# A decode block that streams 88 MB: three loads behind memsets, more idle products, and a scaling split the other way

## The chip, the cores and the metric

The kernel runs on one core of a Trainium2 chip. Its time is the device time of one execution in microseconds (us). Before the change it is 214.62 us, the median of three runs (214.51 to 215.23).

## The reference

One decode step, four tokens (B = 4) of width D = 448, in fp32:

```
h  = x + attention(layernorm(x))            # 16 query heads, 8 k/v heads, Dh = 256
h2 = h + W2 @ gelu(W1 @ layernorm(layernorm(h)) + b1) + b2
```

Attention uses only the last 1024 of the 4096 cached positions, per token and k/v head: `q = layernorm(x) @ wq`, `softmax(q k^T / 16) v`, then `@ wo`. The bulk of the data are the used parts of the k and v caches (each 8 heads x 4 tokens x 1024 x 256 floats, 33.5 MB), read once. With wq, wo, w1 and w2 the kernel reads 88.29 MB. Nothing is reused, so little arithmetic falls on each byte.

## The kernel before, in words

**Loads.** The host packs the inputs so that each load is one rectangle of 128 rows with long rows. Three slots of SBUF (a ring, tag "t") take them in turn. The first slot takes two loads: `first` (the weights wq of head group 0 and a transposed copy of x, 928 KB) and then the rest of `stream0` behind it (4992 KB). Eleven more loads `stream1` to `stream11` of 4 to 7 MB follow, then v of the last head group (`v7`, two parts), wo of the last two groups (`wo67`), w1 (two parts) and w2 (four parts). All of them are issued by SyncE (SP) on one DMA queue, in the order of the program. A load into a slot that was used before waits until its old content has been consumed; the first three slots are free at the start. A small load `rows` (x, b1, b2 by rows, 44 KB) is issued by ScalarE (ACT) on another queue into the tile `rs`.

**Set-up.** VectorE (DVE) and GpSimd (POOL) clear the tiles that later hold the transposed operands: `qT`, `oT` and `pT` (two of each) and `gT`, all with zeros between the used columns. POOL clears these seven in a row (L165), then `rs` (L168), behind which ACT issues `rows`.

**Attention.** For each head group g = 0..7: project q (`pq`, L199), copy it to SBUF (ACT, `qs`, L201) and transpose it with a selecting product (`pqt`, L205); scores (`s`, L219), row maximum (DVE), exponential (ACT), transpose of the probabilities (`ppt`, L244), values (`po`, L256). Then `heads`: the output of values, 128 x (2, 256) in PSUM, is scaled by the softmax's reciprocal into `o`, the first of the two halves by DVE (L273), the second by ACT (L274); four products transpose `o` (`pot`, L281), for column half c = 0, 1 and half i = 0, 1; DVE spreads the result into `oT` (L288), and `project_o` multiplies by wo (`acc` for g < 6, `hsum` for the last two).

**Tail.** From `hsum`: residual, two layer norms, the MLP's first product `pu` (L418, w1), GELU, transpose (`put`), second product `py` (L449, w2), residual, and the store of `res`.

**Idle products.** `keep_warm(n, to)` (L319 to L322) issues n products of a zero tile `idle` (bf16, 32 x 128 times 128 x 512) into a PSUM tile that is overwritten or not read. They stand in the last three head groups and in the tail, where TensorE (PE) would otherwise wait.

The order of work on TensorE is that of the program; the other engines are ordered by a scheduler.

Of the kernel before, what the change touches and what calls it, by code (L numbers as in the profile page):

```python
# [8 lines left out]
F32 = mybir.dt.float32  # L9
# [6 lines left out]
B, D = 4, 448  # L16
HQ, HKV, SK, DH = 16, 8, 4096, 256
REP = HQ // HKV
W = min(4096, max(256, SK // 4))
F = 1792  # L20
P = 128
# [8 lines left out]
WC = 4 * D  # L30
QU = KV // 4
X0 = 64
# [23 lines left out]
def width(part):  # L56
    kind, g, _ = part
    if kind in "kv":
        return QU
    return WC + (X0 if (kind, g) == ("q", 0) else 0)  # L60
# [8 lines left out]
def block_kernel(ctx: ExitStack, tc, rows, first, streams, v7, wo67, w1, w2, out):  # L69
    nc = tc.nc  # L70
# [7 lines left out]
    ps_m = ctx.enter_context(tc.tile_pool(name="ps_m", bufs=2, space=PSUM))  # L78
# [4 lines left out]
    def slot(name):  # L83
        return ring.tile([P, SLOT], F32, tag="t", name=name)

    held = {}
    streams_first = streams[0]

    def part(kind, g, i=0):
        while (kind, g, i) not in held:  # L90
            src = streams.pop(0)
            t = slot("stream")
            wanted = LOADS[len(LOADS) - len(streams) - 1]
            if src is streams_first:
                nc.sync.dma_start(t[:, : WC + X0], first)  # L95
            at = WC + X0 if src is streams_first else 0
            nc.sync.dma_start(t[:, at : at + src.shape[-1]], src)  # L97
            at = 0
            for one in wanted:
                held[one] = t[:, at : at + width(one)]  # L100
                at += width(one)
        return held[kind, g, i]
# [55 lines left out]
    qT = [const.tile([P, 2, B, Q], F32, name=f"qT{i}") for i in range(2)]  # L158
    pT = [const.tile([P, NKC // 2, B, Q], F32, name=f"pT{i}") for i in range(2)]
    oT = [const.tile([P, 4, Q], F32, name=f"oT{i}") for i in range(2)]  # L160
    gT = const.tile([P, NFC, Q], F32, name="gT")
    idle = const.tile([P, 512], BF16, name="idle")
    nc.vector.memset(idle, 0.0)
    for t in qT + oT + pT + [gT]:
        nc.gpsimd.memset(t, 0.0)  # L165

    rs = const.tile([P, 2 * P + FQ], F32, name="rs")
    nc.gpsimd.memset(rs, 0.0)  # L168
# [2 lines left out]
    def spread(t):  # L171
        return t[..., ::GAP]
# [23 lines left out]
    def project_q(g, parts):  # L196
        pq = ps_m.tile([P, 512], F32, tag="m", name=f"pq{g}")
        for j, a, cols, w in parts:
            nc.tensor.matmul(pq[j * Q : (j + 1) * Q, cols], yT[:, a, :], w, start=True, stop=True)  # L199
        qs = work.tile([P, 512], F32, tag="qs", name=f"qs{g}")  # L200
        nc.scalar.copy(qs, pq)  # L201

        pt = ps_m.tile([P, 2 * REP, B], F32, tag="m", name=f"pqt{g}")
        for i in range(2 * REP):
            nc.tensor.matmul(pt[:, i, :], qs[:, i * P : (i + 1) * P], sel[:, :B], start=True, stop=True)  # L205

        src = pt.rearrange("p (r c) b -> p c b r", r=REP)
        for i in range(2):
            nc.vector.tensor_copy(qT[g % 2][:, :, :, i * REP : (i + 1) * REP], src)  # L209

    def scores(g):
        s = [ps_s.tile([P, 512], F32, tag="s", name=f"s{g}_{h}") for h in range(2)]
        if g == HKV - 1:
            keep_warm(12, s[0])
        mx = work.tile([P, 2], F32, tag="mx", name=f"mx{g}")
        for h in range(2):
            for c in range(2):
                for b in range(B):
                    nc.tensor.matmul(  # L219
                        s[h][b * Q : (b + 1) * Q, :], qT[g % 2][:, c, b, :], load_k(g, h, c)[:, b, :],  # L220
                        start=(c == 0), stop=(c == 1),
                    )
            nc.vector.reduce_max(mx[:, h : h + 1], s[h], axis=AX.X)  # L223
        nm = work.tile([P, 1], F32, tag="nm", name=f"nm{g}")
        nc.vector.tensor_max(nm, mx[:, 0:1], mx[:, 1:2])
        nc.vector.tensor_scalar_mul(nm, nm, -SCALE)  # L226
        p = work.tile([P, 2 * 512], F32, tag="p", name=f"p{g}")
        sums = work.tile([P, 2], F32, tag="sums", name=f"sums{g}")
        for h in range(2):
            nc.scalar.activation(  # L230
                p[:, h * 512 : (h + 1) * 512], s[h], AF.Exp, bias=nm, scale=SCALE,
                accum_out=sums[:, h : h + 1],
            )
        rec = work.tile([P, 1], F32, tag="rec", name=f"rec{g}")
        nc.vector.tensor_add(rec, sums[:, 0:1], sums[:, 1:2])
        nc.vector.reciprocal(rec, rec)
        return p, rec

    def transpose_p(g, p):
        pt = ps_t.tile([P, NKC, P], F32, tag="t", name=f"ppt{g}")  # L240
        if g == HKV - 1:
            keep_warm(8, pt.rearrange("p c k -> p (c k)"))
        for c in range(NKC):
            nc.tensor.transpose(pt[:, c, :], p[:, c * P : (c + 1) * P], ident)  # L244

        src = pt.rearrange("p (c i) (b q) -> p c i b q", i=2, b=B)
        for i in range(2):
            nc.vector.tensor_copy(pT[g % 2][:, :, :, i * REP : (i + 1) * REP], src[:, :, i, :, :REP])  # L248
# [21 lines left out]

    def heads(g, po, rec):
        o = work.tile([P, 2, DH], F32, tag="o", name=f"o{g}")
        nc.vector.tensor_scalar_mul(o[:, 0], po[:, 0], rec)  # L273
        nc.scalar.mul(o[:, 1], po[:, 1], rec)  # L274
        pt = ps_m.tile([P, 512], F32, tag="m", name=f"pot{g}")
        if g >= HKV - 3:
            keep_warm(2, pt)
        pt = pt[:, : 2 * REP * B].rearrange("p (c r b) -> p c r b", c=2, r=REP)
        for c in range(2):
            for i in range(2):  # L280
                nc.tensor.matmul(  # L281
                    pt[:, c], o[:, i, c * P : (c + 1) * P], rows_of_pair[:, i * REP : (i + 1) * REP, :],
                    start=(i == 0), stop=(i == 1),
                )
        if g >= HKV - 2:
            keep_warm(1)
        dst = oT[g % 2].rearrange("p (r c) q -> p c r q", r=REP)
        nc.vector.tensor_copy(spread(dst), pt)  # L288
# [30 lines left out]
    def keep_warm(n, to=None):  # L319
        to = tail[0][:, 0, :] if to is None else to  # L320
        for _ in range(n):
            nc.tensor.matmul(to[:Q, :512], idle[:, :Q], idle, start=True, stop=True)  # L322


    p, rec = scores(0)
    project_q(1, wq_parts(part("q", 1)))
    transpose_p(0, p)
    for g in range(HKV):
        if g + 1 < HKV:
            p, rec_next = scores(g + 1)  # L330
            if g + 2 < HKV:
                project_q(g + 2, wq_parts(part("q", g + 2)))
            transpose_p(g + 1, p)
            if g + 1 == HKV - 2:
                keep_warm(8, ps_m.tile([P, 512], F32, tag="m", name="wait"))
            if g + 1 == HKV - 1:
                tail.append(ps_t.tile([P, 2, 512], F32, tag="t", name="tail"))
                accs = once.tile([P, D], F32, tag="u", name="accs")
                nc.scalar.copy(accs, acc)
                keep_warm(10)  # L340
                hsum = ps_s.tile([P, 512], F32, tag="s", name="hsum")[:, :P]
                ph = hsum.rearrange("p (i c) -> p i c", i=2)
                pu = ps_s.tile([P, 512], F32, tag="s", name="pu")[:, :FQ]
                for j in range(4):
                    nc.tensor.matmul(ph[j * Q : (j + 1) * Q], sel, columns(accs, j), start=True, stop=False)
        else:
            v7t = load_v7()
            tw = slot("w1")
            wo_last = [wo_rows(tw[:, i * WC : (i + 1) * WC]) for i in range(2)]
            nc.sync.dma_start(tw[:, : 2 * WC], wo67)  # L350
            tw1 = tw[:, 2 * WC : 2 * WC + W1C]
            for a, n in ((0, 2 * F), (2 * F, W1C - 2 * F)):
                nc.sync.dma_start(tw1[:, a : a + n], w1[:, a : a + n])
            tw2 = slot("w2")
            for c0, n in ((0, 8), (8, 3), (11, 2), (13, 1)):
                nc.sync.dma_start(tw2[:, c0 * D : (c0 + n) * D], w2[:, c0 * D : (c0 + n) * D])  # L356
        if g == HKV - 1:
            keep_warm(4)
        po = values(g, v7t if g == HKV - 1 else None)
        heads(g, po, rec)  # L360
        if g < HKV - 2:
            project_o(g, wo_rows(part("o", g)))
        if g == HKV - 1:
            keep_warm(3)
            for i in range(2):
                project_o(HKV - 2 + i, wo_last[i])
        if g + 1 < HKV:
            rec = rec_next
# [24 lines left out]
    m = row_mean(hs, pm[:, 0:1], "m")  # L393
# [4 lines left out]
    m = row_mean(ds, pm2[:, 0:1], "m2")  # L398
# [128 lines left out]
```

## Time and profile before

| what | value |
|---|---|
| median of three runs | 214.62 us (214.51 to 215.23) |
| the profiled execution: own time / span | 214.47 us / 212.7 us |
| TensorE busy | 147.9 us (70%) |
| VectorE, ScalarE, GpSimd busy | 33.5, 24.1, 5.6 us |
| moved by DMA | 88.52 MB, mean 416 GB/s |
| mean granted TensorE clock | 0.864 |

The span is the profiled part of the execution; 1.8 us of its own time lie outside. Times in the profile are counted from the span's start. In rows of the time-ordered view the columns are: start, duration, engine, line, operation, output<-input, partitions x elements and type, number of instructions, and in brackets how long the engine had been idle before and what ended that. PEld is TensorE loading weights, which overlaps its products. SPq is SyncE issuing a DMA. In the table of stretches a row gives: stretch, its length, busy time and number of instructions for PE, PEld, DVE, ACT and POOL, the granted clock, the mean busy share of the 16 DMA engines, and GB/s. A DMA packet is counted there in the stretch in which it starts, so that a short stretch can show a share above 1, or 0.

### The profile page before, as it was taken

The numbers are of one execution on the slowest core, as the hardware profiler recorded it, in microseconds if no ns is written. First come the engines' busy times: TensorE is split into PE (matmuls) and PEld (weight loads), VectorE is DVE, ScalarE is ACT, GpSimd is POOL, SyncE is SP. The second block draws the span as 40 slices with busy tenths as digits, with TensorE's granted clock in tenths as the row PEclk, the third lists the DMA queues.
The fourth block names the chain that finished last, engine by engine and source line by source line (L and its number), as shares of the span: only waits on it lengthen the run. The fifth ranks groups of instructions, "written<-read, shape, count | busy, mean of one in ns | idle before, by whom it ended". The sixth has DMA issues, their size and how long they took to land.

```text
span 212.7 us, 2616 instructions
## 1 busy us (share of the span) xinstructions
PE 147.9 (70%) x1143; PEld 65.7 (31%) x1143; DVE 33.5 (16%) x138; ACT 24.1 (11%) x57; POOL 5.6 (3%) x17
## 2 busy tenths in 40 slices
PE   0476825842890896870798770687989898999994
PEld 0342311410420622330324130143352434426443
DVE  1410310400112001310104110031130031101220
ACT  1110200300002100210003000030030102000310
POOL 6100000000000000000000000000000000000110
PEclk9999985995578569997559996589699999999999
DMA  7899797989989899998999989999999999999992
GB/s 299 384 466 508 339 508 339 501 383 460 478 367 474 381 466 430 416 481 356 487 392 466 455 384 461 434 434 384 436 411 444 425 434 425 410 417 423 427 386 74
DMA packets 3355, 88.52 MB, mean 416 GB/s; under 512 B 384, under 2 KB 640, under 8 KB 1040
## 3 DMA queue, kind: packets, MB, share of 16 engines
q1 hardware_dynamic: 3312, 88.31, 97.0%
q8 instruction: 9, 0.15, 0.3%
q10 hardware_dynamic: 32, 0.05, 0.1%
q14 instruction: 2, 0.02, 0.0%
HBM read 88.29 MB, written 0.07 MB: 415 GB/s over the span
## 4 chain that ended last, share of the span: by engine, by line
DMA 76%; PE 19%; ACT 1%; DVE 1%; SPq 1%; issue 1%; ACTq 0%
DMA stream<-stream 65%; DMA w<-w 11%; PE s L219 7%; PE po L256 6%; PE ppt L244 2%; PE pq L199 2%; PE pqt L205 1%; PE tail L322 1%; ACT qs L201 1%; PE py L449 0%; ACT p L230 0%; SPq L356 0%; DVE mx L223 0%; SPq L97 0%; SPq L95 0%
## 5 line engine op out<-in xcount | busy, mean ns | idle before, releaser
L219 PE MATMUL s<-stream,qT 128*32 128x512 f32 x256 | 39.3, 762 | 17.8 <-DMA stream<-stream 17.8
L256 PE MATMUL po<-stream,pT 128*32 128x512 f32 x224 | 29.9, 674 | 15.3 <-DMA stream<-stream 15.3
L219 PEld LDWEIGHTS s<-stream,qT 128*32 128x32 f32 x256 | 10.3, 138 | 44.1 <-issue 32.3
L223 DVE TENSOR_REDUCE mx<-s 128x1 f32<-128x512 f32 x16 | 11.1, 692 | 61.5 <-PE s L219 61.5
L256 PEld LDWEIGHTS po<-stream,pT 128*32 128x32 f32 x224 | 6.9, 119 | 31.9 <-DMA stream<-stream 17.9
L199 PE MATMUL pq<-stream,yT 128*32 128x512 f32 (+1 forms) x80 | 10.7, 630 | 7.7 <-DMA stream<-stream 4.8
L281 PE MATMUL pot<-ident,o 128*128 128x8 f32 x64 | 11.3, 287 | 4.7 <-DVE o L273 3.7
L205 PE MATMUL pqt<-sel,qs 128*128 128x4 f32 x64 | 10.1, 281 | 6.1 <-ACT qs L201 6.1
L281 PEld LDWEIGHTS pot<-ident,o 128*128 128x128 f32 x64 | 10.0, 223 | 13.0 <-DVE o L273 11.3
L201 ACT COPY qs<-pq 128x512 f32<-128x512 f32 x8 | 4.7, 586 | 79.5 <-PE pq L199 79.5
L230 ACT ACTIVATE p<-s,nm 128x512 f32<-128x512 f32 x16 | 10.9, 689 | 15.8 <-DVE nm L226 15.8
L205 PEld LDWEIGHTS pqt<-sel,qs 128*128 128x128 f32 x64 | 9.4, 225 | 10.7 <-ACT qs L201 10.7
L273 DVE TENSOR_SCALAR o<-po,rec 128x256 f32<-128x256 f32 x8 | 3.9, 484 | 52.9 <-PE po L256 52.9
L274 ACT ACTIVATE o<-po,rec 128x256 f32<-128x256 f32 x8 | 3.8, 474 | 68.8 <-DVE o L273 68.8
L244 PE MATMUL ppt<-ident,p 128*128 128x128 f32 x64 | 9.8, 299 | 0.4 <-ACT p L230 0.4
L199 PEld LDWEIGHTS pq<-stream,yT 128*32 128x32 f32 x80 | 4.4, 128 | 15.6 <-issue 14.6
L293 PE MATMUL acc<-stream,oT 128*32 128x448 f32 x48 | 7.6, 709 | 2.2 <-DVE oT L288 1.4
L322 PE MATMUL tail<-idle 128*32 128x512 bf16 x33 | 8.5, 381 | 0.4 <-DVE pT L248 0.4
L322 PEld LDWEIGHTS <-idle 128*32 128x32 bf16 x67 | 5.8, 96 | 9.3 <-issue 3.9
L244 PEld LDWEIGHTS ppt<-ident,p 128*128 128x128 f32 x64 | 8.1, 162 | 1.4 <-ACT p L230 1.1
L193 POOL TENSOR_TENSOR r<-ve_r,mhalf 128x1 f32<-128x1 f32 x2 | 1.1, 542 | 191.7 <-DVE ve_r L192 191.7
L209 DVE COPY qT<-pqt 128x16 f32<-128x16 f32 x16 | 2.1, 171 | 20.7 <-PE pqt L205 20.7
(98 smaller groups left out, 70.0 us busy)
## 6 DMA issues: line engine op xcount, KB each, us to landing
stream<-stream SPq DMA_DIRECT2D x5, 7040.0 KB, 40.4
stream<-stream SPq DMA_DIRECT2D x2, 6912.0 KB, 40.6
stream<-stream SPq DMA_DIRECT2D x2, 4992.0 KB, 25.1
stream<-stream SPq DMA_DIRECT2D x2, 4096.0 KB, 24.0
stream<-stream SPq DMA_DIRECT2D x1, 5888.0 KB, 34.4
w<-w SPq DMA_DIRECT2D x2, 1792.0 KB, 23.1
v<-v SPq DMA_DIRECT2D x1, 3072.0 KB, 19.8
w<-wo SPq DMA_DIRECT2D x1, 1792.0 KB, 20.1
```

Source lines behind the costliest of these rows:

```text
L199: nc.tensor.matmul(pq[j * Q : (j + 1) * Q, cols], yT[:, a, :], w, start=True, stop=True)
L201: nc.scalar.copy(qs, pq)
L205: nc.tensor.matmul(pt[:, i, :], qs[:, i * P : (i + 1) * P], sel[:, :B], start=True, stop=True)
L219: nc.tensor.matmul(s[h][b * Q : (b + 1) * Q, :], qT[g % 2][:, c, b, :], load_k(g, h, c)[:, b, :], start=(c == 0), stop=(c == 1),)
L223: nc.vector.reduce_max(mx[:, h : h + 1], s[h], axis=AX.X)
L230: nc.scalar.activation(p[:, h * 512 : (h + 1) * 512], s[h], AF.Exp, bias=nm, scale=SCALE, accum_out=sums[:, h : h + 1],)
L244: nc.tensor.transpose(pt[:, c, :], p[:, c * P : (c + 1) * P], ident)
L256: nc.tensor.matmul(po[b * Q : (b + 1) * Q], pT[g % 2][:, c, b, :], vt[:, :, b, :], start=(c == 0), stop=(c == NKC // 2 - 1),)
L273: nc.vector.tensor_scalar_mul(o[:, 0], po[:, 0], rec)
L281: nc.tensor.matmul(pt[:, c], o[:, i, c * P : (c + 1) * P], rows_of_pair[:, i * REP : (i + 1) * REP, :], start=(i == 0), stop=(i == 1),)
L293: nc.tensor.matmul(acc[i * Q : (i + 1) * Q, :], oT[g % 2][:, i, :], wt[:, i, :], start=(g == 0), stop=(g == HKV - 3),)
L322: nc.tensor.matmul(to[:Q, :512], idle[:, :Q], idle, start=True, stop=True)
```

## The change

Three things are done in one change:

1. The three slots of the ring are taken at the start, and `first` is issued at once. In each slot POOL sets one element to zero, at the place where the slot's next load begins. The loads `stream0`, `stream1` and `stream2` thereby wait for POOL. The memset for `stream0` comes after those of `qT`, `oT` and the first `pT`; the two others after the second `pT` and `gT`. (In the diff, "second to fourth load" are these three, `first` being the first.)
2. Idle products: 3 before the transposes of q of the last head group, 10 for 8 before the transposes of its probabilities, 3 for 2 in each of the last three `heads`, 6 for 4 before the last `values`; and 10 after the last transposes of probabilities become 2 into a tile of their own and 8.
3. In `heads`, DVE scales the first 128 columns of both halves, ACT the last 128 columns of both.

```diff
@@ part @@
             src = streams.pop(0)
-            t = slot("stream")
+            t = first_slots.pop(0) if first_slots else slot("stream")
             wanted = LOADS[len(LOADS) - len(streams) - 1]
-            if src is streams_first:
-                nc.sync.dma_start(t[:, : WC + X0], first)
@@ set-up @@
     nc.vector.memset(idle, 0.0)
-    for t in qT + oT + pT + [gT]:
+    first_slots = [slot("stream") for _ in range(3)]
+    nc.sync.dma_start(first_slots[0][:, : WC + X0], first)
+    for t in qT + oT + pT[:1]:
         nc.gpsimd.memset(t, 0.0)
+    for t, at in zip(first_slots, (WC + X0, 0, 0)):
+        nc.gpsimd.memset(t[:1, at : at + 1], 0.0)
+        if t is first_slots[0]:
+            for later in pT[1:] + [gT]:
+                nc.gpsimd.memset(later, 0.0)
@@ project_q @@
-        pt = ps_m.tile([P, 2 * REP, B], F32, tag="m", name=f"pqt{g}")
+        pt = ps_m.tile([P, 512], F32, tag="m", name=f"pqt{g}")
+        if g == HKV - 1:
+            keep_warm(3, pt)
+        pt = pt[:, : 2 * REP * B].rearrange("p (a b) -> p a b", b=B)
@@ transpose_p @@
-            keep_warm(8, pt.rearrange("p c k -> p (c k)"))
+            keep_warm(10, pt.rearrange("p c k -> p (c k)"))
@@ heads @@
-        nc.vector.tensor_scalar_mul(o[:, 0], po[:, 0], rec)
-        nc.scalar.mul(o[:, 1], po[:, 1], rec)
+        nc.vector.tensor_scalar_mul(o[:, :, :P], po[:, :, :P], rec)
+        nc.scalar.mul(o[:, :, P:], po[:, :, P:], rec)
         pt = ps_m.tile([P, 512], F32, tag="m", name=f"pot{g}")
         if g >= HKV - 3:
-            keep_warm(2, pt)
+            keep_warm(3, pt)
@@ the loop over head groups @@
             if g + 1 == HKV - 1:
+                keep_warm(2, ps_m.tile([P, 512], F32, tag="m", name="wait"))
                 tail.append(ps_t.tile([P, 2, 512], F32, tag="t", name="tail"))
...
-                keep_warm(10)
+                keep_warm(8)
...
         if g == HKV - 1:
-            keep_warm(4)
+            keep_warm(6)
```

How it moves instructions, at the places the prediction speaks of. SyncE at the start of the program, before (`first` is the input named so, `stream` the big loads; the last row shown is the fifth load, which waits for its slot):

```order
L95 DMA stream<-first 128x1856
L97 DMA stream<-stream 128x9984
L97 DMA stream<-stream 128x14080 x2
L97 DMA stream<-stream 128x13824 [waits DMAHW0_49,DMAHW1_49,DVE_49,PE_49]
```

and now:

```order
L163 DMA stream<-first 128x1856
L95 DMA stream<-stream 128x9984 [waits Pool_49]
L95 DMA stream<-stream 128x14080 [waits Pool_49] x2
L95 DMA stream<-stream 128x13824 [waits DMAHW0_49,DMAHW1_49,DVE_49,PE_49]
```

The order is the same; the three loads behind `first` have got a wait for POOL. What POOL does up to there now (`stream` is the single element in a slot):

```order
L165 MEMSET oT_117 128x128
L165 MEMSET pT_114 128x512
L167 MEMSET stream 1x1
L170 MEMSET pT_115 128x512
L170 MEMSET gT 128x448
L167 MEMSET stream 1x1 x2
L173 MEMSET rs 128x704
```

Three one-element memsets have come in between; the order of the others is kept. TensorE in `heads` of the last head group, before (`po` is the output of values, `pot` the transpose of `o`):

```order
L256 MATMUL po_909<-v_893,pT_115 32x512 x3
L322 LDWEIGHTS idle
L322 MATMUL pot_929<-idle 32x512
L322 LDWEIGHTS idle
L322 MATMUL pot_929<-idle 32x512
L281 MATMUL pot_929<-ident,o_926 128x8 [waits DVE_49]
L281 MATMUL pot_929<-ident,o_926 128x8 [waits Activation_49]
L281 MATMUL pot_929<-ident,o_926 128x8 x2
```

and now:

```order
L264 MATMUL po_922<-v_904,pT_115 32x512 x3
L330 LDWEIGHTS idle
L330 MATMUL pot_942<-idle 32x512
L330 LDWEIGHTS idle
L330 MATMUL pot_942<-idle 32x512
L330 LDWEIGHTS idle
L330 MATMUL pot_942<-idle 32x512
L289 MATMUL pot_942<-ident,o_939 128x8 [waits DVE_49]
L289 MATMUL pot_942<-ident,o_939 128x8
L289 MATMUL pot_942<-ident,o_939 128x8 [waits Activation_49]
L289 MATMUL pot_942<-ident,o_939 128x8
```

One idle product more, and two of the four transposes instead of one stand ahead of the wait for ACT.

## The prediction

> **What bounds the kernel now.** I read the page first: the engines' busy time and instructions, the DMA queues (packets, MB, share of the 16 DMA engines) and issues (KB each, us to landing).
>
> ```profile
> PE 147.9 (70%) x1143; PEld 65.7 (31%) x1143; DVE 33.5 (16%) x138; ACT 24.1 (11%) x57; POOL 5.6 (3%) x17
> q1 hardware_dynamic: 3312, 88.31, 97.0%
> q8 instruction: 9, 0.15, 0.3%
> stream<-stream SPq DMA_DIRECT2D x5, 7040.0 KB, 40.4
> stream<-first SPq DMA_DIRECT2D x1, 928.0 KB, 4.8
> rs<-rows ACTq DMA_DIRECT2D x1, 44.0 KB, 7.3
> out<-res SPq DMA_DIRECT2D x1, 64.0 KB, 1.5
> ```
>
> The loads occupy the 16 DMA engines for 97% of the span. A table of stretches shows where the other 3% lie (last two numbers of a row: share of the DMA engines, GB/s):
>
> ```profile
> 1.40:1.60 0.20, 0.00 (x0) 0.00 (x0) 0.20 (x1) 0.00 (x0) 0.20 (x2) 1.00 0.00 0
> 1.60:1.80 0.20, 0.00 (x0) 0.00 (x0) 0.06 (x1) 0.00 (x0) 0.20 (x2) 1.00 1.87 223
> 1.60:3.60 2.00, 0.00 (x0) 0.00 (x0) 0.06 (x1) 0.00 (x0) 2.00 (x7) 1.00 0.79 241
> 20.00:207.00 187.00, 136.67 (x1027) 58.51 (x1022) 28.98 (x110) 22.20 (x55) 1.08 (x2) 0.84 1.00 428
> 208.00:209.00 1.00, 0.96 (x35) 0.69 (x30) 0.00 (x0) 0.00 (x0) 0.00 (x0) 1.00 0.47 163
> ```
>
> From 20 to 207 us the share is 1.00 at 428 GB/s. What is lost lies at the two ends: before the first packets at 1.6 to 1.8, in a slow first 2 us, and in the last 2, where by 208 to 209 half of the engines have finished and the others have not. The chain of waits puts TensorE between the loads, which misleads. Two links near its end:
>
> ```profile
> 183.96 0.33 SPq L356
> 184.80 24.08 DMA w<-w
> ```
>
> SyncE issues w2 when TensorE has freed its slot at 183.96. But 24.08 us pass until it lands, and w2's 3136 KB take 3.21 MB / 428 GB/s = 7.5 us: for some 16.6 us the load stood behind others. The 7040 KB loads say the same: 7.21 MB / 428 GB/s = 16.8 us, and 40.4 us to landing. So these issues could come some 16 us later without harm, and a faster TensorE brings no byte sooner. The end follows the last bytes:
>
> ```profile
> 208.92 0.37 PEld L449 LDWEIGHTS py<-w,gT 128*32 128x32 f32 x16 [0.31 <-DMA w<-w]
> 209.49 0.16 PEld L449 LDWEIGHTS py<-w,gT 128*32 128x32 f32 x8 [0.20 <-DMA w<-w]
> ```
>
> `py` waits twice for w2, 0.31 + 0.20 us; without these waits it would end 0.51 us sooner, so TensorE follows the DMA closely, and the final part of w2 (used at 209.49) sets the end. The price of an edit is therefore what it does to the moment at which the DMA engines run dry.
>
> **The change part by part.** *The waits at the start.* Rows of POOL, SyncE and TensorE, in order of time:
>
> ```profile
> 0.31 0.10 POOL L515 MEMSET const-bfloat16-1.0<- 128x1 bf16 x1
> 0.74 0.36 SPq L95 DMA_DIRECT2D stream<-first  x1
> 1.15 1.71 SPq L97 DMA_DIRECT2D stream<-stream  x3
> 2.00 0.99 POOL L165 MEMSET pT<- 128x512 f32 x2
> 2.94 0.47 POOL L165 MEMSET gT<- 128x448 f32 x1
> 3.35 0.68 POOL L168 MEMSET rs<- 128x704 f32 x1
> 4.07 0.57 ACTq L169 DMA_DIRECT2D rs<-rows  x1
> 5.62 0.57 PE L178 MATMUL pm_x<-stream,mean 128*128 128x12 f32 x2 [5.62 <-DMA stream<-first]
> ```
>
> The first `pT` is done at 2.00 + 0.99/2 = 2.50. A memset of one element isn't in the trace; the nearest row, 128x1, takes 0.10, and below it stands nothing but 0. From POOL's end to a waiting queue's issue: `rs` ends at 3.35 + 0.68 = 4.03 and ACT issues at 4.07, so 0.04. `stream0` is issued at about 2.65 instead of 1.15, 1.5 us later.
>
> Does a DMA engine run dry by it? `first` was issued at 0.74 and its packets begin between 1.60 and 1.80: 0.9 to 1.1 us. The packets of `stream0` can then begin at 3.5 to 3.8. The engines still have `first` until then: its 928 KB are 0.95 MB, and the stretch up to 4.4 reads:
>
> ```profile
> 1.60:4.40 2.80, 0.00 (x0) 0.00 (x0) 0.06 (x1) 0.00 (x0) 2.44 (x7) 1.00 0.88 306
> ```
>
> 2.8 us at 306 GB/s are 0.86 MB of packets begun: at 4.4 there is still some of `first` left. That leaves 0.6 to 0.9 us of cover, and the wait costs nothing. Beyond the cover each microsecond would cost one microsecond, since nothing later catches it up.
>
> Queued behind the waiting instruction on SyncE are `stream1` and `stream2`, released after `gT`: 2.94 + 0.47 + three small memsets, about 3.7, and issued at 3.75 and 4.1. They are needed when 0.95 + 5.11 MB have passed, 14 us after 1.7. POOL's `rs` and with it `rows` move by at most 0.3 us; `rs` is read in the tail, at 196 us. So 0 here.
>
> Can it gain? In the first 2 us the engines move 241 GB/s instead of 428, a shortfall of 0.37 MB or 0.87 us. This is where SyncE hands three big loads to the same engines (1.15 to 2.86). If these hinder `first`, the change frees up to 0.87 us; if the engines merely start slowly, nothing. No row tells the two apart, since no load of this trace starts alone. The bounds are -0.87 and 0; I take -0.1, near 0, because the same SyncE instruction shows no such dip when the first of the five of this merged row is issued at 25.04 into running transfers:
>
> ```profile
> 25.04 69.79 SPq L97 DMA_DIRECT2D stream<-stream  x5
> 24.00:26.00 2.00, 1.29 (x17) 0.59 (x9) 1.01 (x3) 0.95 (x2) 0.00 (x0) 1.00 1.04 451
> ```
>
> One rule of the Trainium skill speaks against the edit: "DMA: Bandwidth & Descriptors", section "Rules for kernel authors", has DMAs issued early, so that their fixed set-up cost overlaps, and its section "Anatomy of one DMA" puts that cost, for DMAs issued by GpSimd, at about 2.0 us, most of it at the end, in the confirmation of the last write. If all 2.0 us lay ahead of the data, the packets of `stream0` would begin at 4.65, and the time by that, an estimate, would be up to 0.3 us more. The trace, with 0.9 to 1.1 us from issue to packets, doesn't agree with so much ahead.
>
> *The idle products and the split.* In `heads` of the last group:
>
> ```profile
> 191.02 0.59 PE L322 MATMUL pot<-idle 128*32 128x512 bf16 x2
> 191.28 0.48 DVE L273 TENSOR_SCALAR o<-po,rec 128x256 f32<-128x256 f32 x1 [5.16 <-PE po L256]
> 191.82 0.39 PE L281 MATMUL pot<-ident,o 128*128 128x8 f32 x2 [0.21 <-DVE o L273]
> 191.86 0.47 ACT L274 ACTIVATE o<-po,rec 128x256 f32<-128x256 f32 x1 [6.85 <-DVE o L273]
> 192.39 0.83 PE L281 MATMUL pot<-ident,o 128*128 128x8 f32 x6 [0.18 <-ACT o L274]
> 193.16 1.04 PE L322 MATMUL tail<-idle 128*32 128x512 bf16 x4
> 194.28 0.16 PEld L299 LDWEIGHTS hsum<-w,oT 128*32 128x32 f32 x8 [0.58 <-DMA w<-wo]
> ```
>
> An idle product adds (1.04 - 0.59) / 2 = 0.22 us. The third one ahead of `pot` fills the 0.21 us for which TensorE waits for DVE: 0 to 0.02. Each transpose is two of the instructions counted here; two of six move ahead of the wait for ACT, and six cost 0.83 against 0.39 for two, 0.11 each, so `pot` ends 0.22 sooner. ACT still waits for DVE. The strided form, 128 x (2, 128), isn't in the trace: 0.48 as the row with 256 columns says, or at most two operations of 128 columns, 2 x 0.29 by the row of `res` below; I take 0.48, since the number of elements is the same, and at 0.58 nearly all of the 0.22 would be gone. All this ends at 194.28, where the weights have waited 0.58 for wo: that load hides the gain, and the loss as well. The other additions:
>
> ```profile
> 156.85 1.06 PE L205 MATMUL pqt<-sel,qs 128*128 128x4 f32 x8 [0.76 <-ACT qs L201]
> 176.19 1.32 PE L244 MATMUL ppt<-ident,p 128*128 128x128 f32 x8 [0.38 <-ACT p L230]
> 187.59 3.64 PE L256 MATMUL po<-v,pT 128*32 128x512 f32 x32 [0.50 <-DMA v<-v]
> 209.99 0.29 DVE L453 TENSOR_TENSOR res<-py,hb 128x128 f32<-128x128 f32 x1 [3.59 <-PE py L449]
> 160.00:207.00 47.00, 43.34 (x385) 19.20 (x385) 7.76 (x30) 6.17 (x15) 1.08 (x2) 1.00 0.99 421
> ```
>
> Three of 0.22 in 0.76 of waiting; two of 0.22 in 0.38, 0.06 over; the ten after `ppt` stay ten; two of 0.22 in the 0.50 for which `po` waits for v7. All but 0.06 us are covered by these waits, and that 0.06 by the 16 us by which w2 queues. Uncovered, all ten would be 2.2 us. The granted clock can't rise where they stand: 1.00 from 160 to 207. Sum: 214.47 of the profiled execution - 0.1 + 0 + 0 = 214.4. The profiled execution lies 0.15 under the median of 214.62, within its runs' spread of 0.72.
>
> **The rivals.** *The start speeds up.* `first` alone on the engines runs at full rate: -0.87 us, 213.6. For it speaks that the slow 2 us coincide with SyncE's three issues; against it the undisturbed stretch at 24 to 26.
>
> *The engines run dry (slower).* It decides if the packets of `stream0` begin later than 4.4, that is over 1.75 us after the issue. The `rows` load takes 7.3 us to landing for 44 KB, so a wait of several us in front of an engine exists here, though behind other packets. With 2.65 us from issue to packets, two and a half times the 1.06 of `first`, they begin at 5.3, and the gap is 0.9 us: 215.4. Against it: `out` lands in 1.5 us in all.
>
> *Instruction packets.* Queue q8 loads instructions on the same engines: 0.3% of 16 x 212.7 us are 10.2 us, for 9 packets 1.1 us each. Ten idle products are 20 instructions more (a weight load and a product each) and move such packets forward. If one falls on the engine that ends last, ahead of its last bytes, w2 lands 1.1 us later: 215.6. Against it: TensorE's 2 x 1143 instructions make one packet for 254, so 20 move the last by a fraction of a microsecond and add at most one, at the end. The Trainium skill, "Runtime: NRT & Kernel Launch", section "Instruction fetch mechanics", says blocks of 256 instructions, fetched ahead and mostly hidden; the trace agrees with the 256, and whether they are hidden from the loads it doesn't say.
>
> **How the numbers follow.** No change that can be measured has 0.57, with its own range from 213.8 to 215.0; the quick start 0.24; engines dry 0.11; instruction packets 0.08. The likeliest gives 214.4. A measurement of this kernel tells about 0.3%, 0.64 us, from no change, that is 213.98 to 215.26. Faster: 0.22 of the quick start and 0.06 of the first case's lower end, 0.28. Slower: 0.09 + 0.07 + 0.01 = 0.17. The rest, 0.55, is the same. The range, 213.4 to 215.5, takes in the quick start with 0.2 to spare and most of the slower cases.
>
> **What would show it.** Right: `stream0` issued near 2.65 and first packets of a load without a stretch under share 0.8 between 3.6 and 5; the final wait of `py` for w2 as before; wo still awaited at `hsum`. Quick start: the stretch 1.6 to 3.6 well above 241 GB/s, and `py`'s last wait near 208.6. Dry engines: a stretch between 4.0 and 5.5 whose share falls, and every later landing late by the same amount. Instruction packets: landings equal until 207, and only the final one late. I am wrong if `py` no longer waits for w2, for then TensorE sets the end.

## The result, and the profile after

The changed kernel takes 216.19 us (median; 215.72 to 216.34) against 214.59 for the kernel before on the same chip: 1.0064 times as long, 95% interval 1.0050 to 1.0079. It is slower, and outside the predicted range. The profiled execution took 215.72 us with a span of 213.8, so the span is 1.1 us longer; the mean granted clock is 0.863 as against 0.864.

The start of the changed kernel, POOL, SyncE and TensorE in order of time (columns as in the prediction; L167 is the one-element memset in a slot):

```profile
2.00 0.52 POOL L165 MEMSET pT<- 128x512 f32 x1
2.46 0.09 POOL L167 MEMSET stream<- 1x1 f32 x1
2.58 1.71 SPq L95 DMA_DIRECT2D stream<-stream  x3
3.37 0.12 POOL L167 MEMSET stream<- 1x1 f32 x2
5.54 0.57 PE L183 MATMUL pm_x<-stream,mean 128*128 128x12 f32 x2 [5.54 <-DMA stream<-first]
18.78 2.79 PE L227 MATMUL s<-stream,qT 128*32 128x512 f32 x12 [2.91 <-DMA stream<-stream]
35.42 1.08 PE L227 MATMUL s<-stream,qT 128*32 128x512 f32 x4 [7.75 <-DMA stream<-stream]
...
210.06 0.37 PEld L458 LDWEIGHTS py<-w,gT 128*32 128x32 f32 x16 [0.35 <-DMA w<-w]
210.64 0.16 PEld L458 LDWEIGHTS py<-w,gT 128*32 128x32 f32 x8 [0.21 <-DMA w<-w]
```

The two rows before that answer to those of 18.78 and 35.42, TensorE's first use of `stream0` and of `stream1`:

```profile
17.67 3.64 PE L219 MATMUL s<-stream,qT 128*32 128x512 f32 x16 [1.72 <-DMA stream<-stream]
34.32 2.74 PE L219 MATMUL s<-stream,qT 128*32 128x512 f32 x9 [6.62 <-DMA stream<-stream]
```

`first` lands as before (5.54, before 5.62). `stream0` lands 1.11 us later (18.78 - 17.67), `stream1` 1.10, and the last part of w2 1.15 (210.64 - 209.49). The landings between, where TensorE waits for them in both traces, are 0.82 to 1.50 us later. So a loss of the final size is there when `stream0` has landed, and the 190 us behind it don't make it good.

Stretches of the changed kernel (the last two numbers: share of the DMA engines, GB/s):

```profile
1.60:3.60 2.00, 0.00 (x0) 0.00 (x0) 0.05 (x1) 0.00 (x0) 2.00 (x10) 1.00 0.86 275
3.60:4.40 0.80, 0.00 (x0) 0.00 (x0) 0.00 (x0) 0.00 (x0) 0.52 (x1) 1.00 1.02 427
4.40:7.40 3.00, 1.17 (x5) 1.08 (x5) 0.53 (x3) 1.28 (x1) 0.00 (x0) 1.00 1.11 419
20.00:207.00 187.00, 140.12 (x1011) 58.08 (x1003) 28.51 (x107) 22.17 (x55) 1.08 (x2) 0.84 1.00 428
```

and the one stretch of the kernel before that isn't in the prediction:

```profile
4.40:7.40 3.00, 1.09 (x5) 1.00 (x5) 0.53 (x3) 1.28 (x1) 0.00 (x0) 1.00 1.06 457
```

From 4.4 to 7.4, where `stream0` follows `first`, the share does not fall in the changed kernel: it is 1.11, even above the 1.06 of before. But the engines move less: GB/s divided by the share, the rate of the 16 engines while they are busy, is 457 / 1.06 = 431 before (as the 428 / 1.00 of the long stretch) and 419 / 1.11 = 377 after. Packets of `stream0` take longer. This quotient is the view in which the loss shows; the share alone doesn't show it, and GB/s alone vary from stretch to stretch, since a packet's bytes and its time are both put down to the stretch in which it starts. The Trainium skill, "Perfetto Trace Analysis", section "Identifying the Most-Contended Engine", says that with 16 engines the busy share of DMA misleads and that HBM utilization, throughput against its peak, should be read in its place; the trace agrees: the share rises from 1.06 to 1.11 while GB/s fall from 457 to 419. The same quotient tells of the start of `first`, 306 / 0.88 = 348 in the prediction's stretch 1.6 to 4.4.

The share hides a second thing, that some engines pause. The changed kernel, and below it the kernel before:

```profile
5.20:5.60 0.40, 0.06 (x1) 0.09 (x1) 0.00 (x0) 0.40 (x1) 0.00 (x0) 1.00 0.32 100
5.60:6.00 0.40, 0.40 (x2) 0.40 (x2) 0.00 (x0) 0.40 (x1) 0.00 (x0) 1.00 0.33 100
```

```profile
5.20:5.60 0.40, 0.00 (x0) 0.01 (x1) 0.00 (x0) 0.40 (x1) 0.00 (x0) 1.00 0.00 0
```

A packet of `stream0` has 39,936 bytes, so 100 GB/s over 0.4 us are one packet; it takes 0.32 x 0.4 x 16 = 2.0 us, the next 2.1, where the steady rate gives 39,936 bytes x 16 / 428 GB/s = 1.5. Both are the first packet of `stream0` on their engine. The trace records the start and length of every packet; what follows is counted from these records, which are in no row shown here. Before, each engine goes from `first` to `stream0` without a pause, the last of them at 5.13. In the changed kernel five of the 16 have ended `first` and wait, 1.4 us in all: their first packets of `stream0` begin at 4.85 to 5.60, which is 2.3 to 3.0 us after the issue. And over all 16 engines the first packet takes 1.85 us instead of 1.49. On the mean of the engines the slow packets are thus the larger part of the loss, and the pauses the smaller.

The mean over the engines isn't the whole of it. The end, after:

```profile
206.00:207.00 1.00, 1.00 (x11) 0.88 (x10) 0.00 (x0) 0.10 (x1) 0.00 (x0) 1.00 0.93 375
207.00:208.00 1.00, 0.62 (x27) 0.65 (x29) 0.45 (x3) 0.00 (x0) 0.00 (x0) 1.00 0.79 315
208.00:209.00 1.00, 1.00 (x47) 1.00 (x39) 0.00 (x0) 0.00 (x0) 0.00 (x0) 1.00 0.51 199
209.00:210.00 1.00, 0.98 (x34) 0.71 (x27) 0.00 (x0) 0.00 (x0) 0.00 (x0) 1.00 0.32 110
210.00:211.00 1.00, 0.94 (x24) 0.53 (x24) 0.00 (x0) 0.00 (x0) 0.00 (x0) 1.00 0.01 2
```

and before (208 to 209 stands in the prediction: share 0.47):

```profile
206.00:207.00 1.00, 0.72 (x30) 0.76 (x33) 0.38 (x3) 0.00 (x0) 0.00 (x0) 1.00 1.00 398
207.00:208.00 1.00, 1.00 (x46) 1.00 (x40) 0.00 (x0) 0.00 (x0) 0.00 (x0) 1.00 0.71 276
209.00:210.00 1.00, 0.92 (x24) 0.45 (x24) 0.01 (x1) 0.00 (x0) 0.00 (x0) 1.00 0.00 0
```

The shares from 206 on add up to 1.00 + 0.71 + 0.47 = 2.18 us before and 0.93 + 0.79 + 0.51 + 0.32 + 0.01 = 2.56 after: the mean engine ends 0.38 us later, the last one more than 1 us (before, no packet begins after 209; after, the share is still 0.32 there). That is near what the start shows: 1.11 x 3.0 us at 377 instead of 431 are 0.42 us for the mean engine, and 1.4 us of pauses over 16 engines 0.09 more. The packet records of `stream0` say the same: the engines end it 0.51 us later on the mean (17.27 against 16.76), and the last one 1.10 us later (18.18 against 17.08). What is paid in time is the last engine's loss. By the Trainium skill, "DMA: Bandwidth & Descriptors", section "Why a DMA increments its semaphore by 16 and not by 1", a load runs on up to 16 engines that finish independently, and only when all have reported has it landed; the rows of this end agree.

The rest of the change did what the prediction says. `heads` of the last group, after:

```profile
192.18 0.81 PE L330 MATMUL pot<-idle 128*32 128x512 bf16 x3
192.98 1.18 PE L289 MATMUL pot<-ident,o 128*128 128x8 f32 x8
193.02 0.47 ACT L282 ACTIVATE o<-po,rec 128x256 f32<-128x256 f32 x1 [6.89 <-DVE o L281]
195.43 1.14 PEld L307 LDWEIGHTS hsum<-w,oT 128*32 128x32 f32 x44 [0.79 <-DMA w<-wo]
```

The third idle product fills the wait for DVE, no wait for ACT is left in front of the transposes, and the weights wait 0.79 us for wo instead of 0.58: the gain of 0.21 has become a longer wait. Queue q8 still has 9 packets.

### The profile page after: what moved, and what is told of

Its sections match the earlier page's. It is cut to its first block, busy times and chain, and to the rows that moved or that the text cites. A ratio compares the mean times of both kernels' runs of the same rounds, so it can differ in the third digit from the quotient of the medians.

```text
span 213.8 us, 2639 instructions
## 1 busy us (share of the span) xinstructions
PE 151.0 (71%) x1153; PEld 65.8 (31%) x1153; DVE 33.5 (16%) x138; ACT 24.0 (11%) x57; POOL 5.7 (3%) x20
## 4 chain that ended last, share of the span: by engine, by line
DMA 81%; PE 15%; POOL 1%; DVE 1%; issue 1%; SPq 0%; POOLq 0%
DMA stream<-stream 69%; DMA w<-w 11%; PE s L227 6%; PE po L264 4%; PE acc L301 2%; PE pot L289 1%; PE pq L204 1%; PE py L458 0%; DVE o L281 0%; SPq L365 0%; POOL qT L165 0%; POOL pT L170 0%; POOL pT L165 0%; POOL gT L170 0%; DVE oT L296 0%
## 5 line engine op out<-in xcount | busy, mean ns | idle before, releaser
L227 PE MATMUL s<-stream,qT 128*32 128x512 f32 x256 | 40.5, 784 | 17.6 <-DMA stream<-stream 17.6
L264 PE MATMUL po<-stream,pT 128*32 128x512 f32 x224 | 31.4, 704 | 16.8 <-DMA stream<-stream 16.8
L213 PE MATMUL pqt<-sel,qs 128*128 128x4 f32 x64 | 10.1, 281 | 5.4 <-ACT qs L206 5.4
L289 PEld LDWEIGHTS pot<-ident,o 128*128 128x128 f32 x64 | 9.1, 207 | 10.7 <-DVE o L281 10.5
L289 PE MATMUL pot<-ident,o 128*128 128x8 f32 x64 | 10.0, 275 | 3.1 <-DVE o L281 3.1
L330 PEld LDWEIGHTS <-idle 128*32 128x32 bf16 x77 | 6.7, 96 | 10.2 <-issue 4.4
L301 PE MATMUL acc<-stream,oT 128*32 128x448 f32 x48 | 6.9, 649 | 2.0 <-DVE oT L296 1.4
```

The lines of the kernel that those rows point to most:

```text
L227: nc.tensor.matmul(s[h][b * Q : (b + 1) * Q, :], qT[g % 2][:, c, b, :], load_k(g, h, c)[:, b, :], start=(c == 0), stop=(c == 1),)
L264: nc.tensor.matmul(po[b * Q : (b + 1) * Q], pT[g % 2][:, c, b, :], vt[:, :, b, :], start=(c == 0), stop=(c == NKC // 2 - 1),)
L289: nc.tensor.matmul(pt[:, c], o[:, i, c * P : (c + 1) * P], rows_of_pair[:, i * REP : (i + 1) * REP, :], start=(i == 0), stop=(i == 1),)
L301: nc.tensor.matmul(acc[i * Q : (i + 1) * Q, :], oT[g % 2][:, i, :], wt[:, i, :], start=(g == 0), stop=(g == HKV - 3),)
```

## The experiments

In the expectations A is that the whole loss comes from the waits at the start, B that instruction packets of the other edits cause it, C that the loss is the time by which `stream0` comes too late behind `first`, D that a `stream0` which comes late costs one fixed amount. F, formed after these, is that what counts is how far ahead of the end of the load before it a load is issued. G, H and I stand with the runs. In each, the kernel before is the base, and all times are medians. Of the edits only the telling lines are shown: those that take the three slots at the start and issue `first`, as in the change, are left out, and `...` marks other cuts.

**The start alone, and the rest alone.** The first run has only the part of the diff with `first_slots`; the second has only the idle products and the split.

> The kernel before with the waits at the start alone. Theory A (DMA engines run dry between `first` and `stream0`; landing of `stream0` was seen at 18.7 us instead of 17.6): all of the loss is here, 215.7 to 216.4 us, TensorE's first wait for `stream0` ends near 18.7. Theory B (instruction packets of the added idle products delay the engine that ends last): the kernel stays at 214.6.

> The changed kernel with the start as before: the idle products and the split alone. Theory A: 214.6, within 0.3%; first wait for `stream0` ends near 17.7 and the last wait for w2 near 209.5. Theory B: 215.7 or more, with landings as before up to 200 us and the last one late by 1.1.

The start alone: 216.40 us, ratio 1.0080 (1.0066 to 1.0093). The rest alone: 214.60, ratio 0.9998 (0.9989 to 1.0007). The rest alone, first use of `stream0`, last wait for w2, and the stretch at the start:

```profile
17.63 3.64 PE L222 MATMUL s<-stream,qT 128*32 128x512 f32 x16 [1.78 <-DMA stream<-stream]
209.55 0.16 PEld L453 LDWEIGHTS py<-w,gT 128*32 128x32 f32 x8 [0.28 <-DMA w<-w]
1.60:3.60 2.00, 0.00 (x0) 0.00 (x0) 0.06 (x1) 0.00 (x0) 2.00 (x7) 1.00 0.82 275
```

The first two are before's times (17.67, 209.49). The loss belongs to the start, the instruction packets are out, and the zero for idle products and split was right.

**The same waits, released early.** POOL clears the element of `stream0` first of all; those of `stream1` and `stream2` follow `gT` as in the change.

```diff
+    nc.gpsimd.memset(first_slots[0][:1, WC + X0 : WC + X0 + 1], 0.0)
     for t in qT + oT + pT + [gT]:
         nc.gpsimd.memset(t, 0.0)
+    for t in first_slots[1:]:
+        nc.gpsimd.memset(t[:1, :1], 0.0)
```

> The kernel before with the same waits of the three loads for GpSimd, but with the one-element memset for `stream0` as GpSimd's first, so that the load is issued about as early as before (1.1 to 1.2 us); the two others come after `gT` (3.5 us). Theory A: it is the lateness and not the wait that costs, 214.6. If the wait itself, or the later issue of `stream1` and `stream2`, cost something, it would stay above 215.2.

214.61 us, ratio 1.0011 (1.0000 to 1.0022). Its SyncE and first use of `stream0`:

```profile
1.14 3.21 SPq L95 DMA_DIRECT2D stream<-stream  x3
17.73 3.64 PE L222 MATMUL s<-stream,qT 128*32 128x512 f32 x16 [1.96 <-DMA stream<-stream]
```

and its stretch behind `first`:

```profile
4.40:7.40 3.00, 1.28 (x5) 1.19 (x6) 0.53 (x3) 1.28 (x1) 0.00 (x0) 1.00 1.07 458
```

458 / 1.07 = 428 GB/s, no slow packets. So neither the waits as such nor the later `stream1` and `stream2` cost anything; the lateness of `stream0` does.

**How late.** The memset for `stream0` at other places: after `rs` (and those of the other two with it), after `oT`, and after `rs` with 2048 columns instead of one element. The three edits against the kernel before, in this order:

```diff
     nc.gpsimd.memset(rs, 0.0)
+    for t, at in zip(first_slots, (WC + X0, 0, 0)):
+        nc.gpsimd.memset(t[:1, at : at + 1], 0.0)
```

```diff
-    for t in qT + oT + pT + [gT]:
+    for t in qT + oT:
         nc.gpsimd.memset(t, 0.0)
+    for t, at in zip(first_slots, (WC + X0, 0, 0)):
+        nc.gpsimd.memset(t[:1, at : at + 1], 0.0)
+        if t is first_slots[0]:
+            for later in pT + [gT]:
+                nc.gpsimd.memset(later, 0.0)
```

```diff
     nc.gpsimd.memset(rs, 0.0)
+    for t, at in zip(first_slots, (WC + X0, 0, 0)):
+        if t is first_slots[0]:
+            nc.gpsimd.memset(t[:, at : at + 2048], 0.0)
...
```

> The kernel before with the three one-element memsets after that of `rs`, so that `stream0` is issued at about 4.1 instead of 2.6 in the changed kernel. Theory A: all engines are dry now, and 1.5 us of lateness beyond the changed kernel cost about 1.5 us: 217.2 to 218.0. Theory B: 214.6.

> The kernel before with the waits at the start, but the memset for `stream0` comes after those of `oT`: issued at about 2.1 instead of 2.6. Theory C (a load that is issued while the engines work reaches the last of them about 3.0 us after its issue, against 1.0 to 1.75 us with idle engines): its last packets begin by 5.1, when the last engine ends `first`, so nothing or little is lost, 214.6 to 215.1. Theory D (any load issued into running engines costs a restart of 0.5 to 1 us on some of them): 215.7 to 216.4.

> As the run with the memsets after `rs`, but that of `stream0` clears 2048 columns, so that it is issued at about 6 us, 1.9 later. Theory C: all engines are dry at 5.1, the packets begin 1.0 to 1.75 after the issue, and each further microsecond costs one: 217.8 to 218.2, first wait for `stream0` to 20.7. Theory D: 216.0 as with the earlier late issue, if only the restart costs.

Issued at 4.10: 215.99 us, ratio 1.0066 (1.0053 to 1.0079). Issued at 2.11: 216.00, 1.0070 (1.0047 to 1.0093). Issued at 5.80: 217.38, 1.0127 (1.0099 to 1.0156). The stretch behind `first` with the issue at 2.11:

```profile
4.40:7.40 3.00, 1.21 (x5) 1.12 (x5) 0.52 (x3) 1.28 (x1) 0.00 (x0) 1.00 1.09 363
```

with 4.10:

```profile
4.40:7.40 3.00, 1.13 (x5) 1.04 (x5) 0.53 (x3) 1.28 (x1) 0.00 (x0) 1.00 0.99 339
```

with 5.80:

```profile
4.40:7.40 3.00, 1.17 (x5) 1.08 (x5) 0.52 (x3) 1.28 (x1) 1.44 (x3) 1.00 0.86 260
```

Only at 5.80 does the share fall below that of the long stretch by much. It hides the pauses here too: with the issue at 4.10 the packet records show the engines idle between `first` and `stream0`, 0.62 us on the mean, and the share is 0.99. An issue half a microsecond earlier than in the change costs as much as one 1.5 us later. So at 4.10 the expectation, made from the lateness, was 1.2 us too high; at 2.11 C is missed by 0.9 us and D's number met; at 5.80 D is missed by 1.4 us and C nearly met. Neither holds over the whole stretch.

**How much work lies ahead.** `first` is made shorter (32 KB: the weights wq move to the front of `stream0`) or longer (2976 KB: two quarters of k of group 0 move into it), with the waits of the change. Short, and then long:

```diff
-    first = np.concatenate([wq[0], xT, np.zeros((P, X0 - ND * B), np.float32)], axis=1)
+    first = np.concatenate([xT, np.zeros((P, X0 - ND * B), np.float32)], axis=1)
...
-    first = np.concatenate([wq[0], xT, np.zeros((P, X0 - ND * B), np.float32)], axis=1)
+    first = np.concatenate([wq[0], xT, np.zeros((P, X0 - ND * B), np.float32), k[0][:, : 2 * QU]], axis=1)
```

> The kernel before with the waits at the start, and wq of group 0 moved from `first` into `stream0`: `first` is 32 KB, so the engines are idle when `stream0` is issued at 2.6. Theory C: idle engines get it within 1.75, by 4.35; `stream0` is 5888 KB now, and the last engine ends it at about 18.6 instead of 17.1: 216.0 to 216.4. If the last engine got it 3.0 us after the issue whether busy or not: 19.9, 217.2 to 217.6.

> The kernel before with the waits at the start, and the first two quarters of k of group 0 moved from `stream0` into `first` (2976 KB instead of 928), so that the engines work on `first` until about 9 us. Theory C: `stream0`, issued at 2.6, is there long before, nothing runs dry, 214.6 within 0.3%. Theory D: 215.7 or more.

Short: 216.90 us, 1.0108 (1.0079 to 1.0136), between the two expectations. Long: 214.98, 1.0021 (1.0008 to 1.0034), near C's number and below D's: with `stream0` issued at 2.61, as in the change, nearly all of the loss is gone once more work lies ahead of it. The same two without the waits:

> No waits; `wq0` moved from `first` to the front of `stream0`, so that `first` is 32 KB and `stream0`, issued at about 1.15, is the first large load on idle engines. Theory F (the slow start belongs to each load that meets an engine with nothing left to do, and takes the issue's 0.41 us later): 0.4 us more than before, 214.9 to 215.3, with the stretch 1.6 to 3.6 below 241 GB/s. Rival (the slow start is one of the engines after a pause, which the 32 KB wake): the dip is over before `stream0`, 214.6 or less.

> No waits; `first` lengthened to 2976 KB by the first two quarters of k0, and `stream0` shorter by these, as in the run with the long `first` and the waits (214.98). If the length of `first` costs nothing: 214.6, and the 0.4 us of that run were of the wait, so even 7 us of work ahead do not hide all. If the division of the loads itself costs: 215.0, and the wait behind a long `first` was free.

Short and free: 215.61 us, 1.0047 (1.0029 to 1.0066), 0.3 above F's expectation. The start of this run:

```profile
1.60:4.40 2.80, 1.20 (x5) 1.11 (x5) 0.58 (x4) 0.00 (x0) 2.45 (x7) 1.00 0.94 281
```

281 / 0.94 = 299 GB/s while busy, less than the 348 of before: a small load ahead doesn't wake the engines for the large one. (This profiled execution is the slowest of the run's eight, 216.54. F's other sign, under 241 GB/s from 1.6 to 3.6, did not come: that stretch reads 393, since all 16 first packets of `stream0`, of 47,104 bytes, begin in it.) Long and free: 215.00 us, 1.0018 (1.0008 to 1.0027). So the 0.4 us of the long `first` belong to this division of the loads, not to the wait, which behind it costs 214.98 - 215.00, nothing.

**A little late, and the two other loads much later.** The memset for `stream0` after those of `qT`; and, with `stream0` as in the change, `stream1` and `stream2` released only after a memset of 128x2048 behind `rs`. The first edit against the start of the change, and of the second the lines that stand there in place of the loop over the slots:

```diff
-    for t in qT + oT + pT[:1]:
+    for t in qT:
...
-            for later in pT[1:] + [gT]:
+            for later in oT + pT + [gT]:
```

```diff
+    nc.gpsimd.memset(first_slots[0][:1, WC + X0 : WC + X0 + 1], 0.0)
+    for later in pT[1:] + [gT]:
+        nc.gpsimd.memset(later, 0.0)
...
     nc.scalar.dma_start(rs[::GAP, :], rows)
+    nc.gpsimd.memset(first_slots[1][:, :2048], 0.0)
+    nc.gpsimd.memset(first_slots[2][:1, :1], 0.0)
```

> The start of the change alone, with the memset that `stream0` waits for put after the two of `qT`: `stream0` issued at about 1.6, between the 1.14 that cost nothing and the 2.1 that cost all (216.0). Theory F (the last DMA engine gets `stream0`'s packets some 3 us after its issue, and a start-up of 1.1 to 1.4 us is paid there as soon as `first` has ended on it): the cost lies between, and grows over the 16 engines one by one: 215.0 to 215.6. Rival (a step: one moment before which nothing is paid and after which all is): either 214.6 or 216.0, within 0.2.

> The start of the change alone, `stream0` issued at 2.6 as there, but `stream1` and `stream2` only at about 6.2, after a memset of 128x2048. Theory F (the cost is `stream0`'s own late start on its last engines): 216.0 to 216.6 as with the start alone (216.4). Rival G (the two issues of SyncE at 3.5, close behind, hold up the descriptors of `stream0`): the cost goes, 214.6 to 215.1.

The first was issued at 1.82 and takes 215.38 us (214.67 to 216.06), ratio 1.0030 (1.0012 to 1.0049): between free and full, as F has it; a step would have left it at one of the two ends. Its executions are spread from the one to the other, 214.67, 214.78, 214.87, 214.96, 215.30 and so on to 216.06; the profiled one, with 215.86, is near the full price. The second takes 216.22, 1.0079 (1.0050 to 1.0109): SyncE's issues close behind `stream0` are not the cause, G is wrong.

**Distance or clock time.** The long `first` again, with `stream0` held back to 5.8 and to 7.9 by a memset of n = 2048 and 4608 columns:

```diff
     nc.gpsimd.memset(rs, 0.0)
+    for t, at, n in zip(first_slots, (WC + X0 + 2 * QU, 0, 0), (2048, 1, 1)):
+        nc.gpsimd.memset(t[:, at : at + n], 0.0)
```

> The long `first` of 2976 KB (free of waits 215.0; with `stream0` issued at 2.6 also 214.98), but `stream0` waits until about 5.8, behind a memset of 128x2048; behind the short `first` an issue at 5.8 cost 2.8 us (217.4). The long `first` should end near 9.3 to 10, 4.9 us later than the short one. Theory F (what counts is how far ahead of the end of `first` the next load is issued, and some 3 us are enough): 3.5 us or more ahead, so free: 214.8 to 215.3. Rival H (the clock time counts: a load issued after 2 us meets something of the program's start, whatever lies ahead of it): 216 or more.

> As the run before, but `stream0` waits until about 8.0, behind a memset of 128x4608: some 1.3 to 2 us ahead of the end of `first`, as `stream0` of the change was (2.6 against 4.4). Theory F: the loss of the change comes back, 1.1 to 1.4 us above 215.0: 216.0 to 216.5. Rival I (only engines that run dry cost, and a load's packets begin 1.06 us after its issue, as the prediction had it): at 9.1, before `first` has ended, so free: 214.8 to 215.3.

Issued at 5.81: 215.06 us, ratio 1.0024 (1.0012 to 1.0036), free beside the 215.00 of this division. Issued at 7.94: 216.72, 1.0086 (1.0057 to 1.0116), the loss of the change again, and somewhat above F's 216.0 to 216.5. The first of the two, in order of time:

```profile
5.81 1.32 SPq L95 DMA_DIRECT2D stream<-stream  x3
11.26 0.57 PE L180 MATMUL pm_x<-stream,mean 128*128 128x12 f32 x2 [11.26 <-DMA stream<-first]
```

and its stretch behind `first`, 5 us later than that of the others:

```profile
9.40:12.40 3.00, 1.09 (x4) 1.00 (x4) 0.01 (x1) 0.00 (x0) 0.00 (x0) 1.00 1.01 432
```

The second:

```profile
7.94 1.28 SPq L95 DMA_DIRECT2D stream<-stream  x3
11.35 0.57 PE L180 MATMUL pm_x<-stream,mean 128*128 128x12 f32 x2 [11.35 <-DMA stream<-first]
```

```profile
9.40:12.40 3.00, 1.05 (x4) 1.00 (x4) 0.00 (x0) 0.00 (x0) 0.00 (x0) 1.00 0.89 338
```

432 / 1.01 = 428 against 338 / 0.89 = 380: the slow packets have moved with the end of `first`. Issued at 5.8, the same load costs 2.8 us behind the short `first` and nothing behind the long one, so H is wrong; issued 3.4 us ahead of the landing of `first`, by which time its packets should long have been there on the prediction's terms, it costs 1.7 us, so I is wrong. What fails in I is the 1.06 us: the packet records show nine of the 16 engines pausing, and the last first packet of `stream0` begins at 10.82 or after, at least 2.9 us after the issue.

**All of them on one scale.** "Ahead" is the time from the issue of `stream0` to the landing of `first` (TensorE's wait for it); "rate" is GB/s over share in the three microseconds behind `first` (from 4.4, with the long `first` from 9.4); "cost" is against 214.6, with the long `first` against its own 215.0. Cost is by medians; ahead and rate are of the one profiled execution.

| `first` | issued | `first` lands | ahead, us | rate, GB/s | cost, us |
|---|---|---|---|---|---|
| long, no waits | 1.16 | 11.23 | 10.1 | 426 | 0 |
| long, waits as in the change | 2.61 | 11.07 | 8.5 | 428 | 0.0 |
| long, held to 5.8 | 5.81 | 11.26 | 5.5 | 428 | 0.1 |
| kernel before | 1.15 | 5.62 | 4.5 | 431 | 0 |
| the rest alone | 1.16 | 5.53 | 4.4 | 428 | 0.0 |
| wait released early | 1.14 | 5.43 | 4.3 | 428 | 0.0 |
| a little late | 1.82 | 5.73 | 3.9 | 385 | 0.8 |
| long, held to 7.9 | 7.94 | 11.35 | 3.4 | 380 | 1.7 |
| after `oT` | 2.11 | 5.51 | 3.4 | 333 | 1.4 |
| the change | 2.58 | 5.54 | 3.0 | 377 | 1.6 |
| `stream1` and `stream2` later | 2.60 | 5.60 | 3.0 | 352 | 1.6 |
| the start alone | 2.59 | 5.52 | 2.9 | 339 | 1.8 |
| after `rs` | 4.10 | 5.59 | 1.5 | 342 | 1.4 |
| short, no waits | 1.15 | 2.52 | 1.4 | - | 1.0 |
| short, waits as in the change | 2.58 | 2.62 | 0.0 | - | 2.3 |
| held to 5.8 | 5.80 | 5.55 | -0.3 | 302 | 2.8 |

With 4.3 us or more the next load costs nothing, whatever the clock time and whatever the size of `first`; at 3.9 half of the price is paid, by the median; from 3.4 down to 1.4 about 1.0 to 1.8 us; below that more. The rate falls where the cost begins.

The packet records, of one execution each, tell why the cost hardly grows between 3.4 and 1.4 us. Issued at 5.80, to idle engines, `stream0` reaches the last engine (its first packet begins there) 1.5 us later, and issued at 4.10, shortly before they end `first`, 1.7 us later, at 5.84. Issued into engines at work it takes longer: at 2.58 it reaches the last engine at 5.60, after 3.0 us, and at 2.11 not before 6.04, after at least 3.9. So over this stretch an earlier issue brings the last engine its packets no sooner.

What stays open: what holds back a load that is issued into working engines; what makes the first packets of such a load slow (the profile tells how long a packet took, not for what it waited); and why the long division costs 0.4 us without any wait. None of the runs beats the kernel before. The start of before with the other edits of the change is the run of the rest alone, and it equals before.

## Why the prediction was wrong

*What bounds the kernel.* Right. The DMA engines set the end; a delay of 1.11 us at `stream0` is found again at the later landings (0.82 to 1.50) and at the final wait of `py` (1.15).

*The issue time.* Right: 2.58, forecast 2.65.

*The cover.* This step failed: "That leaves 0.6 to 0.9 us of cover, and the wait costs nothing." The wait cost 1.15 us in the profiled execution and 1.6 us by the medians. Two things in the step were wrong. It took the 0.9 to 1.1 us between the issue of `first` and its earliest packets, on idle engines, for the time that any load needs. What counts is the last of 16 engines, and these were at work: `stream0` reached five of them only 2.3 to 3.0 us after its issue, when they had ended `first` and stood idle. By the runs some 4.3 us between the issue and the landing of the load ahead are enough, and the change left 3.0. And it put at nothing what the packets themselves lose: the first of `stream0` took 1.85 us on the mean engine instead of 1.49. The sign chosen for dry engines, a falling share, shows neither: the share stayed at 1.02 and 1.11. All the signs that were to show this step right came about, the issue near 2.65, no stretch under a share of 0.8 between 3.6 and 5, the final wait for w2 as before, wo still awaited, and the kernel was slower: these signs could not tell.

*The slow start of `first`.* The price stood in the prediction, 0.87 us in the stretch 1.6 to 3.6, and it was weighed only as something that the change might save. By the runs it is what a load pays when too little lies ahead of it; `first` pays it in every kernel, and in the changed one `stream0` pays it again. The saving isn't shown: the stretch has 275 GB/s instead of 241, but so it has in the run of the rest alone, where SyncE issues the three loads as before. The row of 25.04, quoted as a start without a dip, was no test, since that load had others ahead of it for some 16 us.

*The rivals.* "The engines run dry" had the place, the sign and, with the later landings late as well, the course, and 0.11 was too small a chance for it. Its condition, packets later than 4.4, was met on five engines, at 4.85 to 5.60, about the 5.3 that it reckoned with. Its price of 0.9 us was too low, because it has no slow packets, and the fall of the share that was to show it did not come. The instruction packets cost nothing that can be measured. The bounds for this edit, -0.87 and 0, left the upper side shut on the strength of a cover worked out to a tenth of a microsecond from a row of another load on idle engines.

*Idle products and split.* Right: nothing, 0.9998 times the time, and the 0.2 us by which the weights are ready sooner are waited for wo.

*`stream1` and `stream2`.* Right: released at 3.5 they cost nothing, and released at 5.8 in one run they added nothing to the loss.

*The page's rule.* The rule of the Trainium skill that was set against the edit ("DMA: Bandwidth & Descriptors", "Rules for kernel authors": issue a DMA early, so that its fixed set-up cost overlaps) pointed the right way. The 2.0 us of fixed cost, from the section "Anatomy of one DMA", gave up to 0.3 us by the prediction's estimate; the runs show 1.6 us, and that more than 2.0 us are needed ahead.

## What to carry to other kernels

In a kernel that is bound by its loads, a load needs a lead over the end of the load ahead of it, and that lead isn't the time to the first packet of a load on idle engines: here 4.3 us before that one's landing were enough, and 3.4 cost the full price once and for good. So let nothing stand in front of the second load of such a program, not even a wait of 1.5 us that ends before the load ahead has finished. To see such a loss, divide GB/s by the share of the DMA engines and compare the quotient with the steady one: busy engines can be slow, and a share near 1.00 can hide pauses that are shorter than a packet.

## What the hardware showed that was not expected

- By GB/s over share, busy engines moved only 297 to 364 GB/s in the stretch 1.6 to 4.4 of every kernel, and 302 to 385 behind `first` where the lead was too short, as against 426 to 431 there where nothing was lost. A mean busy share near 1.00 is no proof of full speed.
- A load reached the last of 16 engines 1.5 to 2.0 us after its issue where they stood idle, and 2.9 to 4.2 us or more after it where they were at work on another load and it came too late to follow without a pause.
- At the end of the changed kernel the last engine's loss is about three times the mean one's: 1.15 against 0.38 us.
- At a lead of 3.9 us executions of one program spread from 214.67 to 216.06, all the way from free to full price.
